# One pool of four-tile q and k buffers for both batches, softmax steps moved, and batch 1's scores dealt over block 0

## The chip, the core and the metric

One core of one Trainium2 chip runs the program. The metric is the device time of one execution in microseconds; the kernel before took 1377.85 us, the median of 3 runs (1377.44 to 1380.14).

## What is computed

Two parts in a row, in float32: an attention over channels for each of two batches, and a gated feed-forward layer over all 12032 rows.

```python
B, N, C = 2, 6016, 256; d_ff = 1536
qn = q / (norm(q, axis=1) + 1e-6)              # norms over the 6016 tokens
kn = k / (norm(k, axis=1) + 1e-6)
s  = kn.transpose(0, 2, 1) @ qn / tau          # per batch 256 x 256
a  = softmax(s)
x  = (v @ a).reshape(12032, 256)
xn = x / sqrt(mean(x * x) + 1e-6) * rms_g
g  = xn @ w_gate
out = (silu(g) * (xn @ w_val)) @ w_out
```

## The kernel before

**Tiles.** A batch has 47 tiles of 128 tokens. q and k come in chunks of 1, 2 or 4 tiles (`chunks`), each chunk into one buffer of the pool `raw` (`load_qk`, L155). For a chunk, `scores` (L169) adds its part of k'q to the 256 x 256 product in PSUM (`s`), `squares` (L184) writes the squares of q and k (`sq`) on ACT, and `add_squares` (L195) adds them to `acc` on DVE. A `raw` buffer is free for the next load when both `scores` and `squares` of its chunk are done.

**Stages.** First all of batch 0's chunks. Then a stretch in which the norms of batch 0 are made (`norm_sums`, `norms`, `inverse_norms`, `spread_norms`: pn, nrm, inv and dg, pq and iq), its softmax (z, mx, a), and the first rows of x (px), their normalization (xn), transposes (pxt) and split into two float32r halves (xt). Then 24 blocks, 12 a batch, of 4 tiles each (the last of a batch has 3); a block has 12 steps, f = 0 to 11, one for each 128 columns of d_ff. In a plain step (`emit_hidden`, L608) PE makes pg (gate) and pv (value), ACT a sigmoid, DVE two products (th, hh), ACT and POOL the halves gh and gl of the result, and PE adds `po`, the output product, two steps later (`emit_out`). Blocks 0 and 1 have plain steps only; from block 2 on steps 2 to 7, 10 and 11 are done in pairs with fewer products (`emit_pair`, tiles p and z). Steps 0, 1, 8 and 9 stay plain. The pairs need sums of weights (tile s), which `build_s` (L502) makes in block 1 by way of a working tile `wk`, in three pieces for each of four pairs.

**What lies in block 0 besides.** The weights arrive in blocks of 128 columns (`load_w`, wraw), are decoded on DVE and ACT (`decode_w`: L111, L119, L120, L127) and split into halves on ACT and POOL (`split_w`: L135, L137). Step f decodes block f + 3 and splits f + 2. The scores and squares of batch 1 are also issued in block 0, after a step's own work (`more`): two chunks of 2 tiles in each of steps 0 to 4, one in each later step. What is left of the squares is run after step 11 (`end_block_0`), where PE also makes the norm sums of batch 1 (pn) ahead of block 1.

**Order.** The order on every engine is that in which the program issues; nothing reorders it. All loads and stores are issued from SP's queue in program order; a load whose buffer is still in use holds back those behind it. Batch 1's pool `raw` is opened after batch 0's is closed: 5 buffers of 2 tiles, after 4 buffers of 4 tiles. The squares of batch 1 have one buffer.

**Batch 1's softmax** is issued in block 10 (`B1 - 2`), steps 5 to 9: norms, spread, exp and division in a step each. `emit_pair` and `emit_hidden` use the sigmoid on ACT, so exp needs another function table before it, and the sigmoid's again after it.

Of the kernel before, what the change touches and what calls it, by code (L numbers as in the profile page):

```python
# [8 lines left out]
F32 = mybir.dt.float32  # L9
# [6 lines left out]
P = 128  # L16
# [3 lines left out]
def kernel(  # L20
# [148 lines left out]
    def scores(b, i):  # L169

        t0, n = chunks[b][i]
        r = raw[b, i]
        for t in range(n):
# [10 lines left out]
    def squares(b, i):  # L184

        n = chunks[b][i][1]
        sq = pool["sq"].tile([P, 2, n, C], F32, tag="sq", name=f"sq_{b}_{i}")
        nc.scalar.activation(out=sq, in_=raw[b, i], func=AF.Square)  # L188
        return sq
# [63 lines left out]
    def spread_norms(b, psum, tag):  # L253

        iv, dg = inv[b]
        pq = psum.tile([P, 512], F32, tag=tag, name=f"pq_{b}")
        nc.tensor.matmul(
            out=pq[:, :C], lhsT=ones, rhs=dg.rearrange("p c n -> p (c n)"), start=True, stop=True
        )
        iq = sm_p.tile([P, C], F32, tag="iq", name=f"iq_{b}")  # L260
        nc.scalar.activation(out=iq, in_=pq[:, :C], func=AF.Copy)
        iqs[b] = iq
# [239 lines left out]
    def build_s(p, piece):  # L502
        f0, f1 = 2 * p, 2 * p + 1
        at = [[wgv[0][:, f, c].rearrange("p j m -> p (j m)") for c in range(KC)] for f in (f0, f1)]
        if piece == 0:
            t = pool["wk"].tile([P, 8, 2 * P], F32, tag="wk", name=f"wk_{p}")
            s_tmp[p] = t
            for i, f in enumerate((f0, f1)):
# [3 lines left out]
                )  # L512
        t = s_tmp[p]
        w11, w12, w21, w22, s1, s2, s3, s4 = (t[:, i] for i in range(8))
        q = SP.index(p)
        if piece == 1:
            for o, i0, i1, op in (
                (s1, w21, w22, ALU.add), (s2, s1, w11, ALU.subtract),
                (s3, w11, w21, ALU.subtract), (s4, w12, s2, ALU.subtract),
            ):  # L520
                nc.vector.tensor_tensor(out=o, in0=i0, in1=i1, op=op)  # L521
            nc.scalar.activation(out=s_hl[0][:, q], in_=t[:, 4:7], func=AF.Copy)
            nc.scalar.activation(out=w_hl[0][:, f1, :2 * P], in_=s4, func=AF.Copy)
# [24 lines left out]
    def emit_pair(j, f):  # L548
# [9 lines left out]
        w += [tuple(s[:, SP.index(p), m, k * P:(k + 1) * P] for s in s_hl) for m in range(3)]  # L558
# [49 lines left out]
    def emit_hidden(j, f, between=()):  # L608
# [15 lines left out]
        if j < WINO:  # L624
# [59 lines left out]
    with tc.manual_schedule():  # L684


        phase, plain = ExitStack(), ExitStack()

        def open_pools(stack=phase, side="left", **bufs):
            for name, n in bufs.items():  # L690
                pool[name] = stack.enter_context(
                    tc.tile_pool(name=name, bufs=n, side=side, reuse_waits="tile")
                )

        RAW = 4
        open_pools(raw=RAW, sq=2, acc=1)
        for i in range(RAW):
            load_qk(0, i)
# [19 lines left out]
        for i in range(nch):  # L718
# [7 lines left out]
            if i + RAW < nch:  # L726
                load_qk(0, i + RAW)
# [23 lines left out]
        new_acc(1, 2)  # L751
        nch = len(chunks[1])
        filled = [0, 0]
        waiting = []

        def fill(n=1):
            for i in range(filled[0], min(filled[0] + n, nch)):
                scores(1, i)
            filled[0] = min(filled[0] + n, nch)

        def square(n=1):
            for i in range(filled[1], min(filled[1] + n, nch)):
                waiting.append(squares(1, i))
                raw.pop((1, i))
                if i + RAW < nch:
                    load_qk(1, i + RAW)
            filled[1] = min(filled[1] + n, nch)
# [4 lines left out]

        norms(0)
        fill(2)
        square()
        add()
        inverse_norms(0)
        square()
        spread_norms(0, ps_gv, "gv")
        fill(2)  # L780
        softmax_exp(0, 0)
        softmax_exp(0, 1)
        nc.scalar.activation(out=warm, in_=ones[:, 0:1], func=AF.Sigmoid)
        softmax_div(0, 0)
        softmax_div(0, 1)
        add()
        decode_w(0)
        for h in range(2):
            emit_x(0, h)
            emit_x_squares(0, h)  # L790
# [176 lines left out]
```

## Time and profile before

| | |
|---|---|
| median of 3 runs | 1377.85 us (1377.44 to 1380.14) |
| the profiled execution | 1377.68 us, of which its span is 1375.9 us |
| PE busy | 1322.1 us, 96% of the span |
| DVE, ACT, POOL busy | 1013.4, 645.9, 677.2 us |
| mean granted TensorE clock | 0.981 of full speed |

The page cuts the span in 40 slices; PE is at 90% or more in nearly all of them, and below that in the first eight. DMA is busy for 60 to 90% in the first five slices, and for 10 to 20% behind them.

### The profile page before, as it was taken

The numbers are of one execution on the slowest core, as the hardware profiler recorded it, in microseconds if no ns is written. First come the engines' busy times: TensorE is split into PE (matmuls) and PEld (weight loads), VectorE is DVE, ScalarE is ACT, GpSimd is POOL, SyncE is SP. The second block draws the span as 40 slices with busy tenths as digits, with TensorE's granted clock in tenths as the row PEclk, the third lists the DMA queues.
The fourth block names the chain that finished last, engine by engine and source line by source line (L and its number), as shares of the span: only waits on it lengthen the run. The fifth ranks groups of instructions, "written<-read, shape, count | busy, mean of one in ns | idle before, by whom it ended". The sixth has DMA issues, their size and how long they took to land.

```text
span 1375.9 us, 24750 instructions
## 1 busy us (share of the span) xinstructions
PE 1322.1 (96%) x9420; PEld 1244.3 (90%) x9420; DVE 1013.4 (74%) x1597; ACT 645.9 (47%) x1244; POOL 677.2 (49%) x500
## 2 busy tenths in 40 slices
PE   8877979899999999999989999999999999999998
PEld 7766868799999999999989899999999999999998
DVE  4588956777777777777787787786777776777765
ACT  4354633454454444444544544444445445445432
POOL 1045613355455455455445455555555545545554
PEclk9989989999999999999999999999999999999999
DMA  9666410102102102101102111111111111111010
GB/s 299 225 172 191 145 39 16 31 16 43 35 17 44 35 17 45 33 17 42 33 12 46 29 22 42 32 29 35 32 32 31 32 31 32 34 26 31 20 25 12
DMA packets 150870, 71.61 MB, mean 52 GB/s; under 512 B 109280, under 2 KB 136928, under 8 KB 150752
## 3 DMA queue, kind: packets, MB, share of 16 engines
q1 hardware_dynamic: 150752, 70.04, 20.4%
q8 instruction: 74, 1.21, 0.4%
q14 instruction: 44, 0.36, 0.1%
HBM read 46.40 MB, written 12.32 MB: 43 GB/s over the span
## 4 chain that ended last, share of the span: by engine, by line
PE 85%; DVE 7%; DMA 2%; ACT 2%; issue 1%; SPq 1%; POOL 0%; DVEq 0%; ACTq 0%; POOLq 0%
PE p L568 31%; PE po L659 26%; PE pg L618 9%; PE pv L618 9%; PE s L175 5%; PE px L377 5%; DMA raw<-in_k_dram 2%; DVE acc L197 1%; DVE wx L120 1%; DVE hh L639 1%; SPq L461 1%; DVE wk L521 1%; DVE th L632 0%; ACT sq L188 0%; DMA raw<-in_q_dram 0%
## 5 line engine op out<-in xcount | busy, mean ns | idle before, releaser
L659 PE MATMUL po<-w,gh 128*128 128x256 f32 x2256 | 409.3, 280 | 0.7 <-ACT gh L539 0.7
L659 PEld LDWEIGHTS po<-w,gh 128*128 128x128 f32 x2256 | 352.1, 188 | 10.0 <-ACT gh L539 1.1
L586 POOL TENSOR_TENSOR th<-th,z 128x1024 f32<-128x1024 f32 (+1 forms) x88 | 207.2, 2354 | 226.4 <-ACT th L585 225.9
L659 PE MATMUL po<-w,gl 128*128 128x256 f32 x1128 | 314.9, 279 | 1.4 <-DVE gl L545 1.4
L568 PE MATMUL p<-xt,w 128*128 128x256 f32 (+1 forms) x2112 | 311.2, 282 | 4.8 <-DVE z L632 4.1
L568 PEld LDWEIGHTS p<-xt,w 128*128 128x128 f32 x2112 | 276.5, 190 | 5.9 <-DVE z L632 4.5
L545 POOL TENSOR_TENSOR gl<-z,gh 128x512 fp32r<-128x512 f32 (+1 forms) x88 | 119.3, 1355 | 240.8 <-ACT gh L539 230.1
L600 POOL TENSOR_TENSOR z<-th,z 128x512 f32<-128x512 f32 (+1 forms) x176 | 220.1, 1272 | 12.2 <-DVE z L591 6.9
L568 PE MATMUL p<-xt,s 128*128 128x256 f32 (+1 forms) x1584 | 217.9, 282 | 2.6 <-DVE z L632 2.3
L659 PEld LDWEIGHTS po<-w,gl 128*128 128x128 f32 x1128 | 212.1, 188 | 1.8 <-DVE gl L545 1.8
L539 ACT ACTIVATE gh<-z 128x512 fp32r<-128x512 f32 (+1 forms) x264 | 163.3, 619 | 88.3 <-POOL z L600 78.5
L568 PEld LDWEIGHTS p<-xt,s 128*128 128x128 f32 x1584 | 200.0, 189 | 4.0 <-DVE z L632 3.2
L588 DVE TENSOR_TENSOR z<-p,z 128x512 f32<-128x512 f32 (+1 forms) x176 | 119.4, 678 | 105.2 <-PE p L568 102.0
L618 PE MATMUL pg<-xt,w 128*128 128x512 f32 (+1 forms) x672 | 178.4, 401 | 4.3 <-DVE th L632 3.5
L618 PE MATMUL pv<-xt,w 128*128 128x512 f32 (+1 forms) x672 | 173.4, 393 | 0.0
L580 ACT ACTIVATE z<-p 128x256 f32<-128x256 f32 (+1 forms) x176 | 66.7, 379 | 201.2 <-PE p L568 197.2
L618 PEld LDWEIGHTS pv<-xt,w 128*128 128x128 f32 x672 | 126.9, 189 | 29.4
L618 PEld LDWEIGHTS pg<-xt,w 128*128 128x128 f32 x672 | 120.2, 190 | 26.4 <-DVE th L632 4.8
L591 DVE TENSOR_TENSOR z<-p,z 128x512 f32<-128x512 f32 (+1 forms) x176 | 119.6, 680 | 19.4 <-DVE z L590 1.4
L589 DVE TENSOR_TENSOR z<-p,z 128x512 f32<-128x512 f32 (+1 forms) x176 | 119.6, 680 | 18.3
L629 ACT ACTIVATE z<-pg 128x512 f32<-128x512 f32 (+1 forms) x88 | 51.4, 584 | 161.9 <-PE pg L618 161.3
L545 DVE TENSOR_TENSOR gl<-z,gh 128x512 fp32r<-128x512 f32 (+1 forms) x176 | 117.8, 702 | 5.9 <-ACT gh L539 5.0
(94 smaller groups left out, 1461.0 us busy)
## 6 DMA issues: line engine op xcount, KB each, us to landing
v<-in_v_dram SPq DMA_DIRECT2D x88, 128.0 KB, 3.7
out_dram<-ob SPq DMA_DIRECT2D x88, 128.0 KB, 2.2
xnT<-xw SPq DMA_DIRECT2D x320, 32.0 KB, 1.9
raw<-in_q_dram SPq DMA_DIRECT2D x27, 256.0 KB, 4.4
raw<-in_k_dram SPq DMA_DIRECT2D x27, 256.0 KB, 4.4
raw<-in_q_dram SPq DMA_DIRECT2D x9, 512.0 KB, 5.7
raw<-in_k_dram SPq DMA_DIRECT2D x9, 512.0 KB, 6.6
wraw<-in_moe_w_gate_dram SPq DMA_DIRECT2D x12, 256.0 KB, 2.9
```

The source lines that it names most:

```text
L175: nc.tensor.matmul(out=s_ps[b][:, c, :], lhsT=r[:, 1, t, c * P:(c + 1) * P], rhs=r[:, 0, t, :], start=(t0 + t == 0 and c == 0), stop=(t0 + ...
L377: nc.tensor.matmul(out=px[:, i, :], lhsT=w[:, c, t * P:(t + 1) * P], rhs=x[:, c, :], start=(i == 0 and c == 0 and m == 0), stop=(c == KC - ...
L539: nc.scalar.activation(out=gh, in_=hh, func=AF.Copy)
L545: engine.tensor_tensor(out=gl, in0=hh, in1=f32(gh), op=ALU.subtract)
L568: nc.tensor.matmul(out=t[:, i, :h], lhsT=wm[wi], rhs=xm[xi], start=(i == 0 and q == 0), stop=(q == 2), skip_group_check=True,)
L586: nc.gpsimd.tensor_tensor(out=th[:, :2 * n], in0=th[:, :2 * n], in1=zg[:, :2 * n], op=ALU.mult)
L588: nc.vector.tensor_tensor(out=zz[:, 0:5:4], in0=ps[1], in1=twice(zz[:, 3:4]), op=ALU.add)
L589: nc.vector.tensor_tensor(out=zz[:, 1:3], in0=ps[2], in1=twice(zz[:, 4:5]), op=ALU.add)
L591: nc.vector.tensor_tensor(out=zz[:, 1:3], in0=ps[3], in1=zz[:, 1:3], op=ALU.add)
L600: nc.gpsimd.tensor_tensor(out=o, in0=i0, in1=i1, op=ALU.mult)
L618: nc.tensor.matmul(out=t[:, :n], lhsT=wgv[wi][:, f, c, wj, :], rhs=x[xi][:, c, :n], start=(m == 0), stop=(m == 3 * KC - 1),)
L659: nc.tensor.matmul(out=o_ps[j][t // 2][:, t % 2, :], lhsT=g[:, t * P:(t + 1) * P], rhs=wo[w][:, f, :], start=(f == 0 and t % 2 == 0 and m ...
```

## The change

**Buffers.** Both batches' chunks go through one pool `raw` of 3 buffers of 4 tiles, and `load_next` takes the next chunk of either batch when a buffer is free. Batch 1's chunks have 4 tiles now (before 2); scores and squares still take 2 tiles at a time (`t`, `n`). The second half of a chunk squares into the tile `ob`, which is otherwise used for the output at the end of a block; so the squares of batch 1 have two buffers.

**Order ahead of block 0.** `inverse_norms`, the spread and the copy of iq are issued ahead of the first add of batch 1's squares.

**Block 0.** `more` deals one half chunk to each even step and two to each odd step. v of block 1 is loaded after step 0. The end of the scores (join, norm sums, norms, copy of s) moves into block 1, steps 0 and 1.

**Later.** `build_s` makes its three pieces in three steps that follow each other, with the last in block 2, and its working tile has half the size. The scratch of plain steps comes from z from block 1's step 2 on, and h has one buffer. Batch 1's softmax moves to block 9, steps 6 to 11, with its division in block 10, steps 6 and 7.

```diff
-    for b, sizes in enumerate(([2] + [4] * 9 + [2] * 4 + [1], [2] * 23 + [1])):
+    for b, sizes in enumerate(([2] + [4] * 9 + [2] * 4 + [1], [CH] * 11 + [3])):
...
+        p, tag = (o_p, "ob") if b and t else (pool["sq"], "sq")
+        sq = p.tile([P, 2, n, C], F32, tag=tag, name=f"sq_{b}_{i}_{t}")
+        nc.scalar.activation(out=sq, in_=raw[b, i][:, :, t:t + n, :], func=AF.Square)
...
-            nc.scalar.activation(out=s_hl[0][:, q], in_=t[:, 4:7], func=AF.Copy)
-            nc.scalar.activation(out=w_hl[0][:, f1, :2 * P], in_=s4, func=AF.Copy)
         if piece == 2:
-            nc.vector.tensor_tensor(
-                out=s_hl[1][:, q], in0=t[:, 4:7], in1=f32(s_hl[0][:, q]), op=ALU.subtract
-            )
...
+            for o, x in zip(hi, src):
+                nc.scalar.activation(out=o, in_=x, func=AF.Copy)
+            for o, x, y in zip(lo, src, hi):
+                nc.vector.tensor_tensor(out=o, in0=x, in1=f32(y), op=ALU.subtract)
...
-        RAW = 4
-        open_pools(raw=RAW, sq=2, acc=1)
+        RAW = 3
+        seq = [(b, i) for b in range(B) for i in range(len(chunks[b]))]
+        def load_next():
+            if seq:
+                load_qk(*seq.pop(0))
+        open_pools(both, raw=RAW)
+        open_pools(sq=2, acc=1)
...
-        RAW = 5
-        open_pools(plain, "right", h=2)
-        open_pools(raw=RAW, sq=1, acc=1, wraw=2, wtmp=2)
+        open_pools(sq=1, acc=1, wraw=2, wtmp=2, h=1)
         load_w(0)
-        load_qk(1, 0)
-        load_qk(1, 1)
-        load_qk(1, 2)
         load_w(1)
-        load_qk(1, 3)
-        load_qk(1, 4)
...
-            n = 2 if f < 5 else 1
+            n = 2 if f % 2 else 1
...
+        at(0, 0, lambda: load_v(1))
...
+        at(0, NF - 1, lambda: (square(24), add(24)))
+        at(1, 0, lambda: join_squares(1, 1))
+        at(1, 1, end_scores)
         for p in SP:
             for i in range(3):
-                at(1, 2 * p + 1, lambda p=p, i=i: build_s(p, i))
-        at(1, NF - 1, end_block_1)
...
+                f = 2 * p + 1 + i
+                at(1 + f // NF, f % NF, lambda p=p, i=i: build_s(p, i))
+        at(B1 - 3, 6, lambda: inverse_norms(1))
+        at(B1 - 3, 7, lambda: spread_norms(1, ps_m, "m"))
+        at(B1 - 3, 8, lambda: keep_norms(1))
+        at(B1 - 3, 9, lambda: softmax_min(1, 0))
+        at(B1 - 3, 10, lambda: softmax_min(1, 1))
+        at(B1 - 3, 11, lambda: (softmax_exp(1, 0), softmax_exp(1, 1)))
+        at(B1 - 2, 6, lambda: softmax_div(1, 0))
+        at(B1 - 2, 7, lambda: softmax_div(1, 1))
```

SP's queue at the end of batch 0's loads, before; `raw_0_` and `raw_1_` are chunks of the two batches, `wraw` a block of weights.

```order
L161 DMA raw_0_14_312<-in_q_dram 128x256
L161 DMA raw_0_14_312<-in_k_dram 128x256
L97 DMA wraw_0_372<-in_moe_w_gate_dram 128x2x256
L97 DMA wraw_0_372<-in_moe_w_val_dram 128x2x256
L101 DMA wraw_0_372<-in_moe_w_out_dram 128x512
L161 DMA raw_1_0_376<-in_q_dram 128x512
L161 DMA raw_1_0_376<-in_k_dram 128x512
L161 DMA raw_1_1_379<-in_q_dram 128x512
```

The same place on SP now:

```order
L161 DMA raw_0_14_319<-in_q_dram 128x256
L161 DMA raw_0_14_319<-in_k_dram 128x256
L161 DMA raw_1_0_329<-in_q_dram 128x1024
L161 DMA raw_1_0_329<-in_k_dram 128x1024
L161 DMA raw_1_1_339<-in_q_dram 128x1024
L161 DMA raw_1_1_339<-in_k_dram 128x1024
L161 DMA raw_1_2_346<-in_q_dram 128x1024
L161 DMA raw_1_2_346<-in_k_dram 128x1024
L97 DMA wraw_0_377<-in_moe_w_gate_dram 128x2x256
```

Three chunks of batch 1 with 12 tiles moved ahead of the first weights, into buffers that batch 0 frees.

DVE between the norm sums and the softmax of batch 0, before; `acc_395` is batch 1's sum of squares, `nrm` to `dg` the norms of batch 0.

```order
L228 COPY nrm_397<-pn_342 128x4
L197 TENSOR_TENSOR acc_395<-acc_395,sq_0_408 128x1024
L235 TENSOR_SCALAR nrm_397<-nrm_397 128x2
L238 TENSOR_SCALAR nrm_397<-nrm_397,mtau 128x2
L243 RECIPROCAL inv_416<-nrm_397 128x4
L246 TENSOR_SCALAR dg_418<-ident,inv_416 128x128 x2
```

The same place on DVE now:

```order
L230 COPY nrm_385<-pn_351 128x4
L237 TENSOR_SCALAR nrm_385<-nrm_385 128x2
L240 TENSOR_SCALAR nrm_385<-nrm_385,mtau 128x2
L245 RECIPROCAL inv_402<-nrm_385 128x4
L248 TENSOR_SCALAR dg_404<-ident,inv_402 128x128 x2
L199 TENSOR_TENSOR acc_388<-acc_388,sq_0_0_398 128x1024
```

The add of batch 1's squares moved behind the five steps that make the norms' inverse.

DVE at the change from block 1 to block 2, before; `z_2_0` is block 2's first pair of plain steps, whose products release the PSUM tiles pg and pv, and `wk` and `s` are `build_s`.

```order
L639 TENSOR_TENSOR hh_11_1894<-th_11_1893,pv_11_1886 128x512
L509 TENSOR_TENSOR wk_1914<-w_100,w_101 128x512 x2
L521 TENSOR_TENSOR wk_1914<-wk_1914 128x256 x4
L525 TENSOR_TENSOR s_1352<-wk_1914,s_1351 128x768
L528 TENSOR_TENSOR w_101<-wk_1914,w_100 128x256
L632 TENSOR_TENSOR z_2_0_1944<-z_2_0_1944,pg_0_1930 128x512
L639 TENSOR_TENSOR z_2_0_1944<-z_2_0_1944,pv_0_1937 128x4x4x32
```

The same place on DVE now:

```order
L645 TENSOR_TENSOR z_1_5_1855<-z_1_5_1855,pv_11_1848 128x512
L517 TENSOR_TENSOR wk_1875<-w_100,w_101 128x512 x2
L638 TENSOR_TENSOR z_2_0_1892<-z_2_0_1892,pg_0_1878 128x512
L645 TENSOR_TENSOR z_2_0_1892<-z_2_0_1892,pv_0_1885 128x4x4x32
L368 STREAM_TRANSPOSE vw_1900<-v_1334 128x4x4x32 x2
L531 TENSOR_TENSOR wk_1875<-wk_1875 128x256 x4
L638 TENSOR_TENSOR z_2_0_1926<-z_2_0_1926,pg_1_1912 128x512
L645 TENSOR_TENSOR z_2_0_1926<-z_2_0_1926,pv_1_1919 128x4x4x32
```

Two of the eight `build_s` operations are left ahead of block 2's first products; four stand behind them and the rest behind the second step's.

## Rows read from the trace of the kernel before

**Rows 1.** The page, part 1: busy time, share of the span, instructions.

```profile
PE 1322.1 (96%) x9420; PEld 1244.3 (90%) x9420; DVE 1013.4 (74%) x1597; ACT 645.9 (47%) x1244; POOL 677.2 (49%) x500
```

**Rows 2.** Stretches: us, then PE, PEld, DVE, ACT, POOL busy; PEclk, DMA share, GB/s.

```profile
78.91:190.73 111.82, 87.86 (x436) 75.07 (x437) 91.53 (x88) 57.85 (x86) 52.72 (x29) 0.89 0.50 146
190.73:197.49 6.76, 6.76 (x25) 5.60 (x26) 2.05 (x4) 1.67 (x3) 1.01 (x1) 0.60 0.00 0
197.49:249.60 52.11, 50.05 (x291) 43.19 (x289) 34.62 (x56) 21.20 (x45) 15.66 (x14) 1.00 0.15 31
217.16:225.57 8.41, 8.41 (x51) 7.31 (x49) 4.07 (x8) 3.94 (x11) 3.52 (x4) 1.00 0.00 0
249.60:307.14 57.54, 53.28 (x373) 50.15 (x373) 44.42 (x73) 27.15 (x54) 27.01 (x20) 0.94 0.14 29
307.14:358.03 50.89, 50.89 (x386) 48.67 (x385) 38.50 (x64) 24.38 (x49) 27.49 (x21) 1.00 0.15 32
664.30:720.50 56.20, 52.56 (x382) 48.75 (x381) 45.65 (x80) 26.88 (x53) 26.64 (x21) 1.00 0.13 27
1275.36:1325.54 50.18, 50.18 (x381) 47.97 (x379) 37.04 (x65) 22.81 (x46) 27.35 (x21) 1.00 0.08 20
```

**Rows 3.** PE in order of time: start, us, instruction, [idle before <-releaser].

```profile
59.56 5.42 PE L175 MATMUL s<-raw 128*128 128x256 f32 x16 [6.02 <-DMA raw<-in_k_dram]
...
91.52 3.75 PE L175 MATMUL s<-raw 128*128 128x256 f32 x8 [7.48 <-DMA raw<-in_k_dram]
...
113.45 5.77 PE L175 MATMUL s<-raw 128*128 128x256 f32 x16 [6.79 <-DMA raw<-in_k_dram]
...
189.03 1.84 PE L215 MATMUL pn<-ones,acc 128*128 128x1 f32 x8 [8.56 <-DVE acc L202]
...
205.89 1.59 PE L377 MATMUL px<-a,vt 128*128 128x256 f32 x12
```

**Rows 4.** In order of time, from batch 0's norms to block 0.

```profile
60.67 1.23 DVE L197 TENSOR_TENSOR acc<-acc,sq 128x1024 f32<-128x1024 f32 x1 [6.93 <-ACT sq L188]
...
65.45 0.38 ACT L261 ACTIVATE iq<-pq 128x256 f32<-128x256 f32 x1 [2.46 <-PE pq L257]
...
78.91 2.01 PE L618 MATMUL pg<-xt,w 128*128 128x512 f32 x6 [0.64 <-ACT xt L346]
```

**Rows 5.** DVE in order of time, in block 0.

```profile
92.56 2.28 DVE L197 TENSOR_TENSOR acc<-acc,sq 128x1024 f32<-128x1024 f32 x1
...
134.62 1.84 DVE L127 SCALAR_TENSOR_TENSOR wx<-we,wx 128x768 uint32<-128x768 uint32 x1
...
143.61 1.87 DVE L127 SCALAR_TENSOR_TENSOR wx<-we,wx 128x768 uint32<-128x768 uint32 x1
145.40 1.21 DVE L197 TENSOR_TENSOR acc<-acc,sq 128x1024 f32<-128x1024 f32 x1
...
150.31 1.85 DVE L127 SCALAR_TENSOR_TENSOR wx<-we,wx 128x768 uint32<-128x768 uint32 x1
```

**Rows 6.** SP in order of time: loads of batch 0 chunks.

```profile
23.44 0.33 SPq L161 DMA_DIRECT2D raw<-in_q_dram  x1
...
26.90 0.33 SPq L161 DMA_DIRECT2D raw<-in_q_dram  x1
```

**Rows 7.** The page, part 6: DMA issues, KB each, median us to landing.

```profile
raw<-in_k_dram SPq DMA_DIRECT2D x9, 512.0 KB, 6.6
```

**Rows 8.** DVE and PE in order of time, where block 2 begins.

```profile
254.89 1.29 DVE L509 TENSOR_TENSOR wk<-w,w 128x512 f32<-128x512 f32 x2
...
261.25 1.80 PE L568 MATMUL p<-xt,w 128*128 128x256 f32 x6 [2.58 <-DVE z L632]
```

**Rows 9.** ACT and PE in order of time, at batch 1's softmax in block 10.

```profile
704.07 1.28 ACT L629 ACT_TABLE_LOAD   x1
705.37 0.60 ACT L629 ACTIVATE z<-pg 128x512 f32<-128x512 f32 x1
...
712.88 0.98 PE L568 MATMUL p<-xt,w 128*128 128x256 f32 x6 [1.48 <-DVE z L632]
```

**Rows 10.** POOL in order of time, in block 0.

```profile
91.78 1.98 POOL L545 TENSOR_TENSOR gl<-hh,gh 128x512 fp32r<-128x512 f32 x1
```

More of the change, by code (lines that the diff above doesn't have):

```diff
@@ L167, with scores @@
     acc = {}
-    def scores(b, i):
-        t0, n = chunks[b][i]
+    def scores(b, i, t=0, n=None):
+        t0 = chunks[b][i][0]
         r = raw[b, i]
-        for t in range(n):
+        for t in range(t, t + (n or chunks[b][i][1])):
             for c in range(KC):
@@ L182, in scores, with squares @@
                 )
[L184 to L188, printed above, removed]
+    def squares(b, i, t=0, n=None):
+        n = n or chunks[b][i][1]
+        p, tag = (o_p, "ob") if b and t else (pool["sq"], "sq")
+        sq = p.tile([P, 2, n, C], F32, tag=tag, name=f"sq_{b}_{i}_{t}")
+        nc.scalar.activation(out=sq, in_=raw[b, i][:, :, t:t + n, :], func=AF.Square)
         return sq
@@ L737 @@
         phase.close()
[L741 to L743 removed]
+        open_pools(sq=1, acc=1, wraw=2, wtmp=2, h=1)
         load_w(0)
[L745 to L747 removed]
         load_w(1)
[L749 to L754 removed]
+        parts = [(i, t, min(2, n - t)) for i, (_, n) in enumerate(chunks[1]) for t in range(0, n, 2)]
+        to_score, to_square, waiting = list(parts), list(parts), []
         def fill(n=1):
[L757 to L759 removed]
+            for _ in range(min(n, len(to_score))):
+                scores(1, *to_score.pop(0))
         def square(n=1):
[L762 to L767, printed above, removed]
+            for _ in range(min(n, len(to_square))):
+                i, t, m = to_square.pop(0)
+                waiting.append(squares(1, i, t, m))
+                if t + m == chunks[1][i][1]:
+                    load_next()
         def add(n=1):
@@ L773 @@
         norms(0)
+        new_acc(1, 2)
         fill(2)
         square()
+        inverse_norms(0)
+        spread_norms(0, ps_gv, "gv")
+        keep_norms(0)
+        fill(2)
         add()
-        inverse_norms(0)
+        new_z(0)
         square()
[L779 to L782, printed above, removed]
+        for c in range(KC):
+            softmax_min(0, c)
+            softmax_exp(0, c)
         nc.scalar.activation(out=warm, in_=ones[:, 0:1], func=AF.Sigmoid)
[L784 to L787, printed above, removed]
+        for c in range(KC):
+            softmax_div(0, c)
         for h in range(2):
@@ L790 @@
             emit_x_squares(0, h)
+        add()
+        square()
+        decode_w(0)
         emit_rr(0, 0)
@@ L802 @@
             emit_xT_first(0, h)
+        square()
         decode_w(1)
+        add()
         load_w(3)
-        load_v(1)
+        split_w(1)
         square()
-        split_w(1)
         add()
@@ L810 @@
         load_w(4)
+        square(2)
+        add(2)
         extra = {}
@@ L837, with end_scores @@
             at(0, f, more)
-        def end_block_0():
-            square(nch)
-            add(nch)
-            join_squares(1, 1)
+        at(0, 0, lambda: load_v(1))
+        def end_scores():
             norm_sums(1, acc[1][:, :, 0, :], ps_m, "m")
             norms(1)
+            new_z(1)
+            nc.scalar.activation(out=sm_t[1][0], in_=s_ps[1], func=AF.Copy)
+            s_ps[1] = sm_t[1][0]
             phase.close()
-            s_p = ctx.enter_context(tc.tile_pool(name="s", bufs=1, reuse_waits="tile"))
-            s_hl.extend(s_p.tile([P, len(SP), 3, 2 * P], F32R, name=f"s{i}") for i in range(2))
-            sc = s_p.tile([P, KC, C], F32, name="sc_1")
-            nc.scalar.activation(out=sc, in_=s_ps[1], func=AF.Copy)
-            s_ps[1] = sc
-            open_pools(plain, "right", wk=1)
@@ L853, in end_block_1 @@
-        def end_block_1():
-            plain.close()
-            pool["z"] = ctx.enter_context(tc.tile_pool(name="z", bufs=2, side="right", reuse_waits="tile"))
-        at(0, NF - 1, end_block_0)
+            both.close()
+            for name, n in (("s", 1), ("z", 2), ("wk", 1)):
+                pool[name] = ctx.enter_context(tc.tile_pool(name=name, bufs=n, reuse_waits="tile"))
+            s_hl.extend(
+                pool["s"].tile([P, len(SP), 3, 2 * P], F32R, name=f"s{i}") for i in range(2)
+            )
```

67 lines of the change are left out of this document (29 added, 38 removed).

## The prediction

> **What bounds the kernel now.** I read the page's busy line first: PE is busy for 96% of the span and DVE for 74% [rows 1]. That share is a mean over stages, so I next cut the span at the first gate product of each block [rows 2]. Block 3 is PE alone: 50.89 us, busy for 50.89. Such blocks make up most of the span, and the change leaves their work as it is. Block 0 is another thing: 111.82 us, with PE at 87.86 and DVE at 91.53. Blocks 2 and 10 are longer than their neighbours of the same shape, 57.54 against 50.89 and 56.20 against the 50.18 of block 22. Then I read PE in order of time for its idle stretches: 6.02, 7.48 and 6.79 us behind loads of k, 8.56 behind DVE's sum [rows 3]. After each the clock costs too: sixteen score products take 5.42 or 5.77 us there, against the 3.46 us between two q issues of a four-tile chunk in batch 0 [rows 6], where SP waits for buffers. The loads of batch 1 sit at the end of batch 0 because their buffers open only when batch 0's are closed.
>
> The profiled execution took 1377.68 us, its span 1375.9; it lies 0.17 under the median, so the sum starts from 1377.68.
>
> **The change, part by part.**
>
> *A, up to block 0: -4.1.* PE is idle from 59.56 - 6.02 = 53.54 to 59.56 for the first load of batch 1 [rows 3]. On DVE the first add waits for those squares, 6.93 us, and holds the norms behind it; so iq comes at 65.45 [rows 4]. Now that chunk takes the buffer of batch 0's thirteenth chunk. The last score ends near 53.54 - 1.84 = 51.7 (norm sums as in [rows 3]); three tiles remain after the thirteenth chunk, at 3.46 / 4 = 0.865 each [rows 6], so the load is issued near 49.1. A load takes 6.6 us to land in the backlog [rows 7]; it lands near 55.5, its scores end near 59.0, and iq follows near 59.5: 5.95 earlier. But ACT's squares and an add now stand between weight decoding and the first xn; I give back one decoding step, 1.85 [rows 5], which leaves -4.1. The ends are -2 (an add and a square more in the way) and -7 (nothing given back, and the pause of 0.64 [rows 4] gone).
>
> *B, block 0: -20.6.* The three stalls, 7.48 + 6.79 + 8.56 = 22.8, go if the loads come in time and the end of the scores moves into block 1. The cold clock goes with them: 5.42 - 3.46 = 2.0 for each restart, and the mean granted clock of .89 shows the same [rows 2]. What is late next is DVE. The decoded steps there follow each other at 143.61 - 134.62 = 9.0 us with two adds and 150.31 - 143.61 = 6.7 with one [rows 5]. Two adds cost 6.7 + 1.2 = 7.9 if the wait on the single buffer of squares, which now is two, was the rest; 9.0 is the bound. Nine steps decode a block: five with one add, four with two, 5 x 6.7 + 4 x 7.9 = 65.1. Ahead of these lie two decodings without a step: a plain step costs 4.2 on PE, two of them 8.41 [rows 2], and 6.7 less an add of 1.2 and less 1.3 for its products' waits gives about 4.2 for a decoding as well, so 8.4, with four adds of 1.2 it is 13.2. Transposes of v and the move of x take about 2.2 more, my estimate from the 1.2 us of an add of the same bytes. That is 80.5 from pg at 78.91 - 4.1 = 74.8, so 155.3. Weights split after the last decoding and the step that uses them come behind, 2 x 4.2 = 8, and I allow 3 for hand-overs: block 1 starts near 166, that is 91.2 after pg, 20.6 less than 111.82. PE's floor is lower than that: 87.86 busy, less some 11% of cold clock, about 79. So DVE is the bound and PE waits in small pieces. With adds at the bound (4 x 1.1 more) and hand-overs doubled the gain is 12; at PE's pace with little slip it is 26. Loading v after step 0, the single buffer h and squares into ob I cost at nothing: POOL, which releases h, is busy for 52.72 of 111.82 [rows 2], and ob is idle until the end of the block. If that cover were gone, each would add a wait of the size of a product or two, which is in the 3 allowed.
>
> *C, first step of block 1: -2.5.* It takes 6.76 us at clock .60 [rows 2], after the 8.56 stall; without the stall it is a plain step, 4.2.
>
> *D, sums of weights and the end of scores: -8.0.* Block 1 takes 52.11 with 50.05 busy. It gains the norm sums (under 1 us of PE when warm) and the copies, on ACT with 21.20 busy: about 50.1, -2.0. Block 2 loses 57.54 - 50.89 = 6.65 against block 3; its clock is .94, and its first pair waits 2.58 for z on DVE, where eight wk operations, beginning with 1.29 for the first two, stand ahead [rows 8]. Two now stand ahead, so I take 6.0 of the 6.65. For both the range is -3 (the later pieces collide with block 2's pairs, where DVE has less room: 44.42 of 57.54) to -8.6.
>
> *E, batch 1's softmax: -4.0.* Block 10 is 56.20 - 50.18 = 6.0 longer than block 22. Its waits on z are of 1.48 us, behind a load of the function table of 1.28 [rows 9]. The exp moves next to plain steps' end and the DVE steps apart; two table loads remain, so I keep 2.0 of the 6.0. Ends: 0 (the pairs beside it wait as long) and -6.0. The sigmoid's operation on z starts 0.02 after the table load ends (704.07 + 1.28 = 705.35 against 705.37) [rows 9]: a load alone holds ACT there. The Trainium skill, "ScalarE: Activation LUTs", section "What ACT_TABLE_LOAD costs", adds a drain of about 1.38 us to every change of the set; no such pause shows here, and by that rule two changes would hold ACT 2.8 us longer and E would be about -1.2, the sum 2.8 higher.
>
> *Batch 0's scores with three buffers instead of four: +0.4.* A load must land while two other chunks are scored, 2 x 3.46 = 6.9 us, and lands in 6.6 after the issue [rows 6, 7]; DMA is the stage's limit either way. If it just misses, ten chunks lose 0.4 each: 0 to 4.
>
> Sum: -4.1 - 20.6 - 2.5 - 8.0 - 4.0 + 0.4 = -38.8. 1377.68 - 38.8 = 1338.9, so **1339 us**.
>
> **Rivals.** *DVE's adds fall beside POOL.* An add takes 2.28 us at one place and 1.21 at another [rows 5], the long one, from 92.56 on, begins while POOL runs gl, 91.78 to 93.76 [rows 10]. If the seventeen adds counted above all take the long form, DVE's path grows by 17 x 1.07 = 18 and the time is 1357. For it: DVE is the bound, and spreading puts an add into every step, in which POOL splits weights. Against: in the late steps adds took 1.21. The Trainium skill, "SBUF — State Buffer", section "Who interferes with whom", says that a DVE operation with two SBUF inputs and a POOL operation that reads SBUF exclude each other; the 2.28 against 1.21 agrees, and by that rule it is chance of place which adds are hit.
>
> *The loads come no earlier in effect.* A chunk has 1 MB, twice the former, and SP issues in order: a chunk whose buffer is late holds the weights behind it. Then the waits of A and of the first two loads stay, with their clock: 4.1 + 7.48 + 6.79 + 4 = 22 lost of the 38.8, 1361. For it: three buffers of 4 tiles hold 12 tiles against 10 before, little more, and one load is due per four tiles. Against: DMA's share in block 0 is .50 [rows 2].
>
> *Slower: raw loads behind weights and v.* SP's queue in block 0 mixes raw, weights and v. If a chunk waits for its buffer until ACT has squared its half, and ACT waits for DVE's adds, every chunk may come late as the first two did: (7.48 + 6.79) / 2 = 7.1 of PE, and 2.0 to 2.65 of clock, 9.8 in all. About eight chunks are scored in block 0; it decides from 38.8 / 9.8 = 4 late ones on. With five, 1377.68 - 38.8 + 49 = 1388. For it: one queue and larger pieces. Against: chunks 0 to 2 land during batch 0, and a step of 6.7 to 7.9 us leaves two steps for a load of 6.6.
>
> **How the numbers follow.** Forecast .72, adds beside POOL .14, loads no earlier .10, slower .04. The forecast's parts have ends which, added with their signs as independent terms, give some 11 below and 13 above 1339; the lower end is 1328. The upper goes to 1361, which takes in the two milder rivals, and leaves out the slower one and the tails. A measurement of this kernel tells 0.2%, 2.8 us, from no change. Faster .94: the forecast, the two mild rivals, less a part of the worse mixtures of them; same .02; slower .04.
>
> **What would show it.** A is right if iq comes near 59.5 and the first pg near 75. B is right if PE has no idle stretch above 3 us behind loads of raw, block 1's first pg is near 166, and DVE is busy for over 85% of block 0; it is wrong in size if adds there take 2.28 or more, wrong in kind if score products still wait for raw. C and D are right if block 1 and 2 take about 50 and 51.5 at a clock of 1.00, with no wait on wk's place; E if blocks 9 and 10 together are about 2 longer than plain ones. Batch 0's part is wrong if scores there wait for k more than now. The whole is wrong if the loads of raw stand on SP for more than two steps behind a buffer.

## The result, and the profile after

The changed kernel takes 1358.72 us, the median of 4 runs (1357.24 to 1360.36), where the kernel before took 1377.64 beside it; the ratio is 0.9859, with an interval of 0.9841 to 0.9877. That is 18.9 us less, in place of the 38.8 that the prediction summed. The profiled execution took 1357.24 us with a span of 1355.5, 20.4 less than the one before.

The page's busy line of the changed kernel, which answers to [rows 1]:

```profile
PE 1316.0 (97%) x9420; PEld 1237.2 (91%) x9420; DVE 1019.0 (75%) x1601; ACT 645.2 (48%) x1248; POOL 672.4 (50%) x500
```

The span is cut at the first gate product of a block, as in [rows 2]; the columns are the same. The lines are block 0, the first step of block 1, block 1, block 2, block 3, and blocks 9 and 10:

```profile
75.71:174.96 99.25, 85.38 (x428) 71.78 (x429) 86.73 (x86) 56.93 (x86) 50.45 (x29) 0.97 0.55 165
174.96:179.34 4.38, 4.38 (x27) 3.81 (x25) 3.18 (x4) 1.07 (x3) 0.89 (x1) 1.00 0.00 0
174.96:232.36 57.40, 54.81 (x322) 47.78 (x320) 40.64 (x64) 23.01 (x51) 17.10 (x16) 1.00 0.14 28
232.36:288.00 55.64, 50.83 (x373) 47.59 (x374) 45.08 (x73) 27.30 (x55) 26.36 (x20) 1.00 0.14 30
288.00:338.87 50.87, 50.87 (x386) 48.67 (x385) 38.84 (x64) 24.37 (x49) 27.84 (x21) 1.00 0.15 32
593.51:646.64 53.13, 52.10 (x388) 49.26 (x387) 43.86 (x72) 25.74 (x51) 27.32 (x21) 1.00 0.13 28
646.64:699.65 53.01, 50.98 (x380) 48.10 (x379) 44.83 (x74) 25.63 (x52) 27.58 (x21) 1.00 0.14 28
```

The whole gain lies in the five places that the prediction named, and in each it is smaller:

| stretch | before | after | gain | predicted |
|---|---|---|---|---|
| up to the first gate product | 78.91 | 75.71 | 3.2 | 4.1 - 0.4 |
| block 0 | 111.82 | 99.25 | 12.6 | 20.6 |
| block 1, first step included | 58.87 | 57.40 | 1.5 | 2.5 + 2.0 |
| block 2 | 57.54 | 55.64 | 1.9 | 6.0 |
| blocks 9 and 10 | 107.38 | 106.14 | 1.2 | 4.0 |

(58.87 is 6.76 + 52.11 of [rows 2]; block 9 of before took 51.18.) The gains add to 20.4, which is the difference of the spans. In block 0 no product waits for a load any more. What PE waits for there, by the view of waits (us in total, times, longest):

```profile
PE pxt L451 <- DVE xt L357: 4.4, 1, 4.4
PE pg L624 <- DVE th L638: 3.9, 2, 3.2
PE px L386 <- ACT xn L427: 2.6, 1, 2.6
PE pg L624 <- POOL w L137: 2.1, 3, 1.1
PE px L386 <- POOL vt L351: 0.6, 1, 0.6
PE pg L624 <- ACT xt L355: 0.6, 1, 0.6
```

The two long waits for raw, 14.3 us, and the 8.56 for the norm sums [rows 3] have gone, and 14.2 of others stand there. So the questions are what sets block 0's pace now, and why the three later parts brought so little.

DVE's own waits say what the change did to it. Before, in block 0:

```profile
DVE acc L197 <- ACT sq L188: 11.9, 10, 1.6
```

and in the changed kernel:

```profile
DVE vw L368 <- DMA v<-in_v_dram: 3.4, 1, 3.4
DVE acc L199 <- ACT sq L190: 2.4, 2, 1.6
```

With a second buffer for the squares DVE no longer stands still ten times for them. DVE was busy for 91.53 and idle for 20.3 in that block; it is busy for 86.73 and idle for 12.5 now. 4.8 less work and 9.5 less waiting for squares, against 3.4 for v, make 10.9 of block 0's 12.6. Of the 11.9 us, 5.6 stood in the steps that decode weights (five waits of 1.1) and 6.2 behind the last decoding, among the squares left over. Up to the end of the last decoding the block is 5.0 shorter (86.85 before, 81.90 now), and behind it 7.6 (24.97 and 17.35). This balance is read from two traces; no run took the second buffer away alone, or went back to chunks of two tiles.

The two long waits for raw reached DVE much shortened. Before, the first product behind each (th) waited on DVE for

```profile
98.27 0.69 DVE L632 TENSOR_TENSOR th<-th,pg 128x512 f32<-128x512 f32 x1 [1.08 <-ACT th L629]
...
121.30 0.69 DVE L632 TENSOR_TENSOR th<-th,pg 128x512 f32<-128x512 f32 x1 [2.13 <-ACT th L629]
```

that is 1.08 and 2.13 us, where PE had stood still for 7.48 and 6.79.

### The profile page after: what moved, and what is told of

The parts are those of the page before. It is cut to its first block, busy times and chain, and to the rows that moved or that the text cites. A ratio compares the mean times of both kernels' runs of the same rounds, so it can differ in the third digit from the quotient of the medians.

```text
span 1355.5 us, 24741 instructions
## 1 busy us (share of the span) xinstructions
PE 1316.0 (97%) x9420; PEld 1237.2 (91%) x9420; DVE 1019.0 (75%) x1601; ACT 645.2 (48%) x1248; POOL 672.4 (50%) x500
## 4 chain that ended last, share of the span: by engine, by line
PE 80%; DVE 10%; DMA 3%; issue 3%; SPq 2%; ACT 2%; POOL 0%; DVEq 0%; ACTq 0%; POOLq 0%
PE p L574 30%; PE po L665 25%; PE pg L624 9%; PE pv L624 9%; PE px L386 5%; PE s L175 3%; DMA raw<-in_k_dram 2%; SPq L470 1%; DVE wx L127 1%; DVE wx L120 1%; DVE wk L531 1%; DVE z L638 1%; DVE acc L199 1%; DMA v<-in_v_dram 1%; DVE xp L491 1%
## 5 line engine op out<-in xcount | busy, mean ns | idle before, releaser
L551 POOL TENSOR_TENSOR gl<-z,gh 128x512 fp32r<-128x512 f32 (+1 forms) x98 | 132.1, 1348 | 270.6 <-ACT gh L545 249.1
L606 POOL TENSOR_TENSOR z<-th,z 128x512 f32<-128x512 f32 (+1 forms) x176 | 219.5, 1269 | 18.4 <-DVE z L597 9.9
L545 ACT ACTIVATE gh<-z 128x512 fp32r<-128x512 f32 (+1 forms) x274 | 169.7, 620 | 119.5 <-POOL z L606 84.1
L624 PE MATMUL pg<-xt,w 128*128 128x512 f32 (+1 forms) x672 | 178.0, 399 | 10.9 <-DVE z L638 4.2
L635 ACT ACTIVATE z<-pg 128x512 f32<-128x512 f32 (+1 forms) x98 | 57.1, 584 | 166.4 <-PE pg L624 166.2
```

The lines of the kernel that those rows point to most:

```text
L545: nc.scalar.activation(out=gh, in_=hh, func=AF.Copy)
L551: engine.tensor_tensor(out=gl, in0=hh, in1=f32(gh), op=ALU.subtract)
L606: nc.gpsimd.tensor_tensor(out=o, in0=i0, in1=i1, op=ALU.mult)
L624: nc.tensor.matmul(out=t[:, :n], lhsT=wgv[wi][:, f, c, wj, :], rhs=x[xi][:, c, :n], start=(m == 0), stop=(m == 3 * KC - 1),)
```

## The experiments

Each kernel is the changed one with one edit, but for two further down that join several. Between kernels whose code is the same up to there, block 0 began at anything from 73.0 to 76.7 us, so small differences are read from the lengths of blocks, and the times stand beside them. Block 0 itself, where four kernels issue the same in it (the changed one and three with later edits alone), took 98.85 to 100.03.

**Without the additions of squares in block 0.**

```diff
                 for _ in range(n):
                     square()
-                    add()
+                    waiting.clear()
```

> Leaves out the additions of batch 1's squares that are issued in the steps of block 0 (16 of the 24; batch 1's norms are then too small); the squares themselves, loads and scores stay. Theory: DVE sets the pace of block 0; without some 20 us of its 87 PE is the bound, whose busy time there is 85.4 with some cold clock in it: block 0 between 82 and 89, time 1342 to 1348. Rival: PE waits in block 0 for weights split on POOL, for v, or for raw, whatever DVE does: block 0 96 to 99, time 1355 to 1359.

It took 1346.62 (1342.81 to 1347.63). Its block 0:

```profile
73.14:161.61 88.47, 83.21 (x429) 70.55 (x429) 66.15 (x70) 56.83 (x86) 49.03 (x29) 0.98 0.60 185
```

DVE's work fell by 20.6, the block by 10.8, and now PE fills 83.21 of 88.47. DVE sets the pace of block 0 in the changed kernel; where it doesn't, PE does.

**Loads of batch 1 late again.**

```diff
-            load_next()
+            if seq[0][0] == 0:
+                load_next()
...
         load_w(0)
+        load_next()
+        load_next()
         load_w(1)
+        load_next()
```

> No chunk of batch 1 is loaded until batch 0's last product is issued: first the first weights, then two chunks of 4 tiles, weights, and a third chunk; buffers, their sizes and all orders else are as in the changed kernel. Theory of the prediction: the early loads bring the gain of the stretch ahead of block 0 and of the first part of block 0: the first score products of batch 1 wait 5 to 7 us again, block 0 begins 3 to 6 later, PE waits for raw again for over 8 us in all, time 1366 to 1375. Rival: the place of the norms on DVE and the even deal do it, and DVE's own pace hides late loads: block 0 begins within 1.5 of 75.7 or makes it up, time 1358 to 1362.

It took 1367.47 (1363.96 to 1368.33), 8.8 more. PE waits for the first chunk again:

```profile
61.04 5.23 PE L175 MATMUL s<-raw 128*128 128x256 f32 x16 [6.85 <-DMA raw<-in_k_dram]
```

Block 0 begins at 80.90 instead of 75.71. The theory's half on this stretch holds. Its other half falls: block 0 itself takes 98.5, and no product waits for raw in it. The profiled execution was the fastest of its four, 6.7 longer than that of the changed kernel: 5.2 of it ahead of block 0, and 2.2 in block 11 (48.37 against 46.19), which takes from 46.2 to 49.6 in the profiles of kernels in which nothing was edited near it; block 0 gives 0.75 back. The 2.1 between the 6.7 and the 8.8 of the medians aren't explained by the one profile.

**Batch 1 dealt from the front again.**

```diff
-            n = 2 if f % 2 else 1
+            n = 2 if f < 5 else 1
```

> Undoes only the even deal of batch 1 over block 0: two half chunks in each of steps 0 to 4, one in each later step, as before the change, with the new buffers and early loads. Theory: the even deal is what took the waits for raw out of block 0 (with the loads late, none came back there): dealt from the front, scores overtake the loads, waits for raw of over 4 us in all come back in block 0, block 0 takes 101 to 108, time 1361 to 1367. Rival: the larger buffers and DVE's pace leave time for the loads either way: waits for raw under 1.5 in block 0, which takes 98 to 100.5, time 1357 to 1360.

1357.67 (1355.78 to 1360.19). Of the theory only the mechanism came. PE's waits in block 0:

```profile
PE s L175 <- DMA raw<-in_k_dram: 8.7, 3, 5.4
PE pxt L451 <- DVE xt L357: 2.5, 1, 2.5
PE px L386 <- ACT xn L427: 2.3, 1, 2.3
```

The waits for raw are back, 8.7 us, and the block takes 98.65, no longer than with the even deal (99.25). They replace PE's waits for DVE. So the even deal takes away a wait and no time.

**The norms behind the first add again.**

```diff
         square()
+        add()
         inverse_norms(0)
...
         fill(2)
-        add()
         new_z(0)
```

> Undoes only the order on DVE ahead of block 0: the first add of batch 1's squares stands ahead of the steps that make batch 0's inverse norms again; the early loads stay. Theory: the loads did the work of this part: the add waits for squares that come with the first score products now, and costs its own 1.2 to 2.5 us: block 0 begins at 76.5 to 78.5, time 1359 to 1361. Rival: the new place on DVE is what brings the norms forward, by half or more of the 5 us: block 0 begins at 79 to 81, time 1362 to 1364.

1358.83 (1357.68 to 1361.75); block 0 begins at 75.00, earlier than the theory's 76.5 and within the spread named above. The add doesn't wait for squares now, but 2.12 us for POOL's zeroing of its sum, and behind it the product that spreads the norms waits on PE:

```profile
60.14 0.67 PE L259 MATMUL pq<-dg,ones 128*128 128x256 f32 x2 [1.04 <-DVE dg L248]
```

iq, the copy of this product, comes 5.44 us after the first score of batch 1. In seven other kernels whose first sixteen scores take 3.69 or 3.70, as here, it comes after 4.16 or 4.17. So the order on DVE is worth some 1.3 us, too little for the times to show; in the changed kernel's own profile those scores took 5.38, and iq came after 5.85.

**The end of batch 1's scores ahead of block 1 again.**

```diff
-        at(0, NF - 1, lambda: (square(24), add(24)))
-        at(1, 0, lambda: join_squares(1, 1))
-        at(1, 1, end_scores)
+        at(0, NF - 1, lambda: (square(24), add(24), join_squares(1, 1), end_scores()))
```

> Undoes only the move of the end of batch 1's scores: the join of the sums, the norm sums on PE, the norms and the copy of s stand behind step 11 of block 0 again, ahead of block 1's first product; all else as in the changed kernel (its blocks 0 and 1 together 156.65). Theory: this move is the largest single part of what block 0 gained, since DVE's pace hides the loads and the deal: PE waits 3 to 6 us for the join, the norm sums run cold and the first step of block 1 too: blocks 0 and 1 together 161.5 to 167, time 1363 to 1369. Rival: DVE is late behind block 0 anyway and the wait only moves from later steps: 156 to 159, time 1357.5 to 1361.

1363.28 (1362.49 to 1364.06), 4.6 more. Blocks 0 and 1 take 161.52 against 156.65:

```profile
73.32:176.79 103.47, 87.20 (x436) 73.24 (x437) 88.70 (x88) 57.43 (x87) 51.40 (x29) 0.95 0.54 158
176.79:182.64 5.85, 5.85 (x27) 4.91 (x26) 2.18 (x5) 1.15 (x2) 1.01 (x1) 0.71 0.01 1
```

The first step of block 1 stands at a clock of .71 again, 5.85 instead of 4.38. The 4.9 agree with the theory's low end and with the times, whose ranges don't meet, but not all of them stand where the edit is. From the last decoding to block 1 it is 18.87 against 17.36, and block 1 is 0.65 longer; the other 2.7 lie ahead of that, where both kernels issue the same, and where DVE waited longer for v. Of the waits in this kernel, DVE's and PE's:

```profile
DVE vw L368 <- DMA v<-in_v_dram: 6.1, 1, 6.1
```

```profile
PE pn L217 <- DVE acc L204: 2.0, 1, 2.0
```

So the stretches show 2.2 for the move; against the 15.7 that the part behind the last decoding takes in other profiles it is 3.9. PE waits 2.0 for the join where it waited 8.56 before, less than the theory's 3 to 6.

**v of block 1 early, and x's transposes a step later.** In the changed kernel DVE stands still for v; and PE waits for x behind the last decoding. First both places as they were (DVE, then PE, in order of time):

```profile
103.70 1.31 DVE L368 STREAM_TRANSPOSE vw<-v 128x512 f32<-128x512 f32 x2 [3.44 <-DMA v<-in_v_dram]
```

```profile
158.54 0.84 PE L451 MATMUL pxt<-ident,xn 128*128 128x128 f32 x4 [4.40 <-DVE xt L357]
```

```diff
-        at(0, 0, lambda: load_v(1))
...
         load_w(4)
+        load_v(1)
```

> v of block 1 is loaded ahead of block 0 again, behind the weights of step 4, and nothing else differs from the changed kernel (1358.7, its block 0 99.25). Theory: DVE sets the pace of block 0, and in the changed kernel it stands still for 3.44 us for this load (transposes of v at 103.70), PE for 3.22 behind it. Both waits go, all behind them comes some 3.4 earlier: block 0 about 95.9, time about 1355.3. Rival: another engine sets the pace there, or DVE's delay is made up before the end of the block: block 0 within 0.7 of 99.25, time 1358 to 1359.

```diff
-            8: (lambda n: emit_xT_first(n, 0),),
-            9: (lambda n: emit_xT_first(n, 1),),
+            9: (lambda n: emit_xT_first(n, 0),),
+            10: (lambda n: emit_xT_first(n, 1),),
```

> The two halves of block 1's transposes of x are issued in steps 9 and 10 of block 0 instead of 8 and 9; else the changed kernel. Theory: PE idles 4.40 us there (158.54) because the operation that takes the first half out of PSUM stands on DVE behind the last decoding of weights; a step later no decoding stands ahead of it. The wait goes and with it the slow clock after it (17 score products in 5.4 us where 3.7 would do): block 0 shorter by 4 to 6, 93 to 95, time about 1353.5. Rival: DVE is late by itself, and PE waits as long for products of steps 9 to 11 instead: block 0 98 to 99.5, time 1357.5 to 1359.

Block 0 takes 95.52 and 94.94, as both theories had it, 3.7 and 4.3 less; the times are 1353.42 (1351.25 to 1357.34) and 1353.13 (1351.53 to 1357.42). Both edits in one:

> v of block 1 loaded ahead of block 0, and the transposes of x in steps 9 and 10: both of the parts that took 3.7 and 4.3 from block 0's 99.25 alone. Theory: they are separate waits in one chain: block 0 90.5 to 92, time about 1350. Rival: the earlier v already shortened the wait for x (2.78 instead of 4.40), and DVE's pace sets the rest: block 0 92.5 to 95.5, time 1351.5 to 1353.5.

1350.80 (1350.43 to 1351.44), ratio to the kernel before 0.9805 (0.9792 to 0.9818), clear of the changed kernel's. Its block 0:

```profile
73.82:166.25 92.43, 85.18 (x428) 72.26 (x429) 86.60 (x85) 55.59 (x84) 49.88 (x28) 0.96 0.59 177
```

Together they save 6.8 of 8.0, between theory and rival by the block's length. DVE is busy for 94% of the block. This is the fastest of the kernels that compute the whole; its median is below those of both, and its block 0 is 2.5 shorter than the shorter of theirs.

**The sums of weights.** First all three pieces of a sum in one step, as before the change:

```diff
-                f = 2 * p + 1 + i
+                f = 2 * p + 1
```

> Undoes only the spread of the sums of weights: all three pieces of a sum in one step again (3, 5, 7, 11 of block 1), in the new form and the small working tile. Theory: the spread itself was worth little (block 2's gain was the clock, .94 to 1.00, and its waits are as long as before: 4.8 us against 4.3): blocks 1 and 2 together within 2 of 113.0, time 1357.5 to 1361. Rival, as predicted: the spread is worth 6 of block 2's 6.65: blocks 1 and 2 together 117 to 120, time 1363 to 1366.

1359.15 (1358.13 to 1360.26). Blocks 1 and 2:

```profile
176.71:233.10 56.39, 55.08 (x323) 47.85 (x321) 39.79 (x64) 23.55 (x51) 17.50 (x16) 1.00 0.14 29
233.10:289.71 56.61, 52.29 (x373) 48.81 (x374) 44.24 (x73) 27.31 (x55) 26.67 (x20) 0.97 0.14 29
```

Together 113.00, against 113.04 with the spread. It moved 1.0 from block 2 into block 1 and saved nothing. Then all of them early:

```diff
-        for p in SP:
+        for m, p in enumerate(SP):
             for i in range(3):
-                f = 2 * p + 1 + i
+                f = 2 * m + 2 + i
```

> The three pieces of each of the four sums of weights start in steps 2, 4, 6 and 8 of block 1 instead of 3, 5, 7 and 11, so that the last is done ahead of block 2; else the changed kernel (its block 1 57.40, block 2 55.64; blocks of PE alone would be 54.3 and 50.9). Theory: in the changed kernel the last sum still stands on DVE ahead of the products that release PSUM for block 2's first steps and pairs (waits of PE of 1.45, 1.58, 2.42, 0.45 and 0.37 us from 232 to 251): they go but for 1.6 that the split of x makes, and blocks 1 and 2 together fall from 113.0 to 107.5 to 109.5, time 1353.5 to 1355.5. Rival: the eight operations cost the same wherever they stand, since DVE has no room among block 1's steps 8 to 10, with x's transposes: together 112 to 114, time 1357.5 to 1359.5.

1365.81 (1365.20 to 1368.42), slower, and the experiment was badly built: a sum's third piece replaces weights in place, and here step 11 of block 1 reads the replaced ones, so this kernel computes with other weights there, and waits for them:

```profile
PE pg L624 <- ACT w L534: 13.1, 1, 13.1
```

PE had run ahead of DVE and loses that lead at once. In block 2 behind it, with no sums left, PE waits for nothing, and the block takes 49.67. With the third piece held behind step 11, on top of the two edits that gained:

```diff
+        when = dict(zip(SP, ((2, 3, 4), (4, 5, 6), (6, 7, 8), (9, 11, 12))))
...
-                f = 2 * p + 1 + i
+                f = when[p][i]
```

> The same with the sums of weights moved within what they may: pieces of the four sums in steps 2-3-4, 4-5-6, 6-7-8 of block 1, and of the last in steps 9 and 11 and in step 0 of block 2 (it changes weights that step 11 reads, so its third piece stays behind that). Theory: what costs in blocks 1 and 2 is that pieces of the sums stand on DVE ahead of the products that release PSUM at the change of block, together with the split of x: blocks 1 and 2 together fall from 113.0 to 108 to 110.5, time 2.5 to 5 under that without it. Rival: DVE's sum of work over these steps sets it wherever the pieces stand: 112 to 114, time as without it.

1352.99 (1350.90 to 1353.35), not below 1350.80. Blocks 1 and 2 take 58.61 + 54.85 = 113.5 against 57.41 + 55.46 = 112.9 without it. The rival holds: three placings, 112.9 to 113.5, and the changed kernel's placing alone took 112.8 to 113.6 in the profiles of the other kernels.

**Batch 1's softmax in block 10 again.**

```diff
-        at(B1 - 3, 6, lambda: inverse_norms(1))
-        at(B1 - 3, 7, lambda: spread_norms(1, ps_m, "m"))
...
-        at(B1 - 2, 7, lambda: softmax_div(1, 1))
+        at(B1 - 2, 5, lambda: inverse_norms(1))
+        at(B1 - 2, 6, lambda: (spread_norms(1, ps_m, "m"), keep_norms(1)))
+        at(B1 - 2, 7, lambda: [go(1, c) for c in range(KC) for go in (softmax_min, softmax_exp)])
+        at(B1 - 2, 8, lambda: softmax_div(1, 0))
+        at(B1 - 2, 9, lambda: softmax_div(1, 1))
```

> Undoes only the place of batch 1's softmax: norms, spread, exp and division in steps 5 to 9 of block 10 again; else the changed kernel (its blocks 9 and 10 together 106.1; without softmax they would be 101.1). Theory from the two traces: the move spread the same DVE and ACT work over two blocks and saved 1.2: together 106.8 to 108, time 1359.5 to 1361. Rival, as predicted: the move is worth 4: together 109.5 to 111, time 1362 to 1364.

1357.34 (1356.74 to 1364.23). Blocks 9 and 10 take 50.89 + 56.09 = 106.98, 0.84 more than in their new place, where every other kernel's profile has 106.13 to 106.16. The time doesn't show it.

## Why the prediction was right, and where it was too large

The place was right in all five terms, and the range held the time; four sizes were too large, and block 0's is 8.0 of the 18.4 us that went missing between 38.8 and 20.4. That the range held is in part luck: the parts' own ends reach 13 above 1339, to 1352, and it was stretched to 1361 for two rivals that did not come true. Nor do these ends follow from the parts: added as independent terms they give some 6.5 below and 11.5 above, and 11 below is their plain sum.

*A, 4.1 less 0.4 for batch 0: 3.2 came.* The early loads are the cause (late again: block 0 5.2 later), as worked out. The norms' place on DVE adds some 1.3 to it at most. That the add "holds the norms behind it" was misread: before, DVE had made dg by 62.84, and its product pq began on PE at 64.82, behind sixteen scores [rows 3]:

```profile
62.36 0.48 DVE L246 TENSOR_SCALAR dg<-ident,inv 128x128 f32<-128x128 f32 x2
```

```profile
64.82 0.59 PE L257 MATMUL pq<-dg,ones 128*128 128x256 f32 x2
```

iq came at 61.55, 3.9 earlier, not 5.95, for the same reason. The scores began when they should (55.70, where the working has 55.5 and its terms, 49.1 + 6.6, give 55.7), but took 5.38 in place of 3.5, at a granted clock of .68:

```profile
55.70:61.08 5.38, 5.38 (x17) 4.42 (x18) 2.70 (x6) 1.03 (x1) 1.93 (x2) 0.68 1.02 361
```

In eight of the other profiles they take 3.69 or 3.70, and iq comes between 58.87 and 60.85, about where 59.5 was forecast. Batch 0 itself ends 1.9 later with three buffers (its last norm sum 55.47 against 53.54), within the 0 to 4 and above the 0.4; it cost nothing here, since batch 1's first chunk landed no earlier. Of the 1.85 given back for a decoding step 0.7 was due: from iq to the first gate product it takes 14.16 now and took 13.46 (78.91 - 65.45 of [rows 4]).

*B, 20.6: 12.6 came.* That DVE would be the next limit is shown (no additions: 10.8 less). So is its pace: th comes 6.69 us after the one before it where one add lies between, and 7.99 and 8.01 where two do, against 6.7 and 7.9 in the working (DVE in order of time):

```profile
129.30 0.67 DVE L638 TENSOR_TENSOR th<-th,pg 128x512 f32<-128x512 f32 x1
...
137.29 0.68 DVE L638 TENSOR_TENSOR th<-th,pg 128x512 f32<-128x512 f32 x1
...
143.98 0.68 DVE L638 TENSOR_TENSOR th<-th,pg 128x512 f32<-128x512 f32 x1
...
151.99 0.68 DVE L638 TENSOR_TENSOR th<-th,pg 128x512 f32<-128x512 f32 x1
...
155.76 1.85 DVE L127 SCALAR_TENSOR_TENSOR wx<-we,wx 128x768 uint32<-128x768 uint32 x1
```

The last decoding ends at 157.61, where 155.3 and the 0.9 of the later start had 156.2; the wait for v is in it, so the rest of the working was some 2 too long. Two steps failed. "Loading v after step 0 ... I cost at nothing": it cost 3.44 of DVE (loaded early: block 0 3.7 shorter), and 3.8 to 6.1 in five profiles of kernels that issue the same up to there. The order on SP's queue would have told it: v now stands behind a chunk of 1 MB and in front of DVE's transposes a step later. Its issue began at 94.72, and it had landed at 103.6. And the tail, "2 x 4.2 = 8, and I allow 3": 157.61 to 174.96 is 17.4 (15.7 to 17.2 in three other profiles of the same block). Behind the last decoding stood the operation that takes x out of PSUM, and PE waited 4.40 for it. Then it had transposes and sixteen scores still to do, at a granted clock of .69, and two whole steps with scores at 1.00; the working's tail held no scores:

```profile
158.54:164.00 5.46, 5.46 (x21) 4.62 (x21) 3.83 (x6) 3.02 (x5) 3.91 (x2) 0.69 0.00 0
164.00:174.96 10.96, 10.96 (x62) 9.54 (x61) 5.98 (x7) 4.10 (x7) 1.67 (x2) 1.00 0.01 2
```

With x's transposes moved off the decoding and v early the tail is 12.6 (153.63 to 166.25). The raw waits, which the working counted as gains because PE's row shows them, were not worth their length: the 7.48 and 6.79 reached DVE as 1.08 and 2.13, and dealt from the front such waits come back for 8.7 us at no cost. In its sums the working also rounds 2 x 4.2 + 3 down to 11, and its low end, 4.4 and 3 less than 20.6, would be 13, not 12. Put back one at a time, the late loads, the deal from the front and the late norms leave block 0 at 98.5 to 98.84, and the end of the scores gives 2.2 to 4.9 over blocks 0 and 1; which part of the change brought the rest of the 12.6 isn't isolated. The second buffer fits best: steps with two adds came 9.0 apart before and come 8.0 apart now.

*C, 2.5: right.* The first step takes 4.38 instead of 6.76, at a clock of 1.00; with the end of the scores put back it takes 5.85 at .71.

*D, 2.0 and 6.0: -0.9 and 1.9.* The mechanism fell, not only the size. "Two now stand ahead, so I take 6.0": the other operations only stand ahead of the next products, and DVE's four take 2.62. The changed kernel in order of time, DVE and PE:

```profile
241.68 2.62 DVE L531 TENSOR_TENSOR wk<-wk 128x256 f32<-128x256 f32 x4
244.22 0.68 DVE L638 TENSOR_TENSOR z<-z,pg 128x512 f32<-128x512 f32 x1
```

```profile
244.95 0.98 PE L574 MATMUL p<-xt,s 128*128 128x256 f32 x6 [2.42 <-DVE z L638]
```

The 2.42 is the 2.58 of [rows 8] in a new place. Block 1 stays 3.1 above the 54.3 which its plain steps, the norm sums and two x products come to (12 x 4.2 + 1.0 + 2 x 1.45). What blocks 1 and 2 did gain, 3.4, comes from the slow clock: 2.4 in the first step and 2.45 of PE's busy time in block 2 (53.28 before [rows 2], at .94, and 50.83 now, at 1.00), less 0.9 in the rest of block 1 and 0.55 of longer waits in block 2. That block 2's clock had been low was in the row, and was read as a sign of the stall alone.

*E, 4.0: 1.2 came,* and 0.84 by the run that put it back. "I keep 2.0 of the 6.0" kept too little. Blocks 9 and 10 together are 106.14 against 50.89 + 50.18 = 101.1 without softmax: 5.1 remain, 3.1 of them PE's idle time and 2.0 its longer busy time. PE's waits in them add to 3.2, against 3.7 in block 10 before. ACT in order of time at the exp:

```profile
645.55 1.28 ACT L289 ACT_TABLE_LOAD   x1
646.84 0.51 ACT L289 ACTIVATE z<-z,mx 128x256 f32<-128x256 f32 x1
...
648.30 1.28 ACT L635 ACT_TABLE_LOAD   x1 [0.36 <-PE pg L624]
649.59 0.60 ACT L635 ACTIVATE z<-pg 128x512 f32<-128x512 f32 x1
```

After either load the next operation starts within 0.02. The Trainium skill, "ScalarE: Activation LUTs", section "What ACT_TABLE_LOAD costs", gives a drain of some 1.38 us besides; these rows don't show it, so that the prediction's 1.2 by that rule is met in number, not in cause. The cause of the 5.1 wasn't isolated.

*The rivals.* Adds beside POOL didn't decide: 20 adds in block 0 took 1326 ns in the mean, 1347 before. Of the decoding, L111 rose from 7.7 to 10.7 us, while L120 fell from 20.1 to 14.6. The Trainium skill, "SBUF — State Buffer", section "Who interferes with whom", names both kinds as ones that can collide with POOL, and these sums agree: it is place that decides which line is long. That loads would come no earlier, or late for many chunks, did not happen. The time is near the first rival's 1357 for another reason.

## What to carry to other kernels

A wait in the row of the engine that looks like the bound is worth its length only if the engine behind it isn't nearly as late: before counting PE's waits, read the waits of the next engine in the same stretch. Here PE's 14.3 us of waits for loads reached DVE as 3.2, while DVE stood still for 11.9 us for squares in a single buffer. And before an order is changed on one engine, look at what its last result waits for on the next: here the norms were ready 2 us before PE could use them. Work moved in front of another consumer of the same engine is not removed; a step of it is gained only where that engine has idle time at the new place. And an operation that is moved and "costs nothing" needs its consumer looked up: here a load one step ahead of its reader cost 3.4 us or more.

## What the hardware showed besides

The same elementwise operation on DVE takes its time or twice to three times that, by what POOL does beside it: L111 from 0.55 to 1.61 and L120 from 0.94 to 2.01, in block 0 of one execution. There the nine long ones of these 22 (1.04 and more) began while an operation of POOL was running, and the thirteen short ones (0.96 at most) while POOL was idle or within 0.06 us of being so. And the first gate product came between 73.0 and 76.7 us in profiles of kernels that issue the same work up to it, so a start behind a stretch of loads isn't known to better than some 4 us from one profile. A part of it is the clock: sixteen scores ahead of it took 3.69 at a granted clock of 1.00 and 5.38 at .68, in kernels that issue the same.
